# From octet 2 on: every product as two outputs on two 64-row halves of the array

## The chip, the cores and the metric

The kernel runs on one core of one Trainium2 chip. Five engines work side by side and meet through semaphores: TensorE (PE; its weight loads are listed apart as PEld), VectorE (DVE), ScalarE (ACT), GpSimd (POOL) and SyncE (SP), which here only issues transfers. The metric is the device time of one execution in microseconds (us), shown as the median of several runs. The profile is of one execution; its span reaches from the first to the last instruction of the program.

## The reference

A token mixer and an MLP read the same normalised input, and both results are added to the input (S = 2048 tokens, D = 448, 16 heads of 28, F = 1792):

```python
xn = layernorm(x)
# branch A, "hedgehog" linear attention
q, k, v = split(xn @ wqkv)                        # 16 heads of 28
phi_q = concat(softmax(q @ w_phi), softmax(-q @ w_phi))   # per head, 56 wide
phi_k = the same of k
kv  = phi_k^T @ v          # per head, 56 x 28, summed over all tokens
z   = sum over tokens of phi_k
A   = ((phi_q @ kv) / (phi_q . z + 1e-6)) @ wo
# branch B
h   = gelu(layernorm(xn) @ w1)                    # 448 columns in four groups of 112
hs  = (groups of h moved by +1, -1, +2, -2 tokens) @ w2
x1  = xn + hs
B   = x1 + gelu(layernorm(x1) @ w3) @ w4
out = x + A + B
```

## The kernel before

The tokens are 16 tiles of 128. A helper class, `Recorder`, takes down every operation in the order in which the Python code names it, works out which operation must wait for which from the memory that they touch (`solve`), and then hands each engine its own operations in that order. So the order of the calls is the order on every engine, and an engine that waits holds up all that was recorded behind it. All matrix products have the line of the helper `mm` (L188), transposes on TensorE that of `tr` (L192), ScalarE's work that of `act` (L196), VectorE's and GpSimd's that of `ew` (L200).

*Contraction over 448 rows.* Weights and transposed activations lie in four overlapping blocks of 128 rows that begin at rows 0, 128, 192 and 320. The product for an even tile takes blocks 0, 3 and 2 whole (`full`) and the upper 64 rows of block 1 (`tail`), one for an odd tile blocks 0, 3 and 1 and the lower 64 rows of block 2. That is three and a half passes over the array. `batch` puts the tails of several outputs next to each other, so that those of an even and an odd tile use the two halves of the array.

*Accumulators.* There are eight banks, `banks[0]` to `banks[7]`, used in pairs by `two(b)`. Each call names its bank. `nxt` turns three pairs over for k and q, and w2's products of the tiles 4 to 7 have the single banks 6 and 7 in turn.

*The stages.* `octet(g)` handles four tiles g of v and of w1 (`v_pair`, `w_pair`), 0 and 1 first, then 2 and 3 with the folds between. A fold multiplies w_phi into the weights of k or q (`fold`), 112 columns a product. `w2_tile` makes w2's product of four groups of 112 rows, adds it into `xn` on VectorE (`w2_add`) and takes the statistics of the sum there. Then `ks` and `qs` make phi(k) and phi(q): each pair of tiles ends in two exps on ScalarE (scale +1 and -1), and `k_norm` sums and inverts per head on VectorE and multiplies on GpSimd. `kv_tile` accumulates kv over all tokens with 64-column weights, two at once. `chunks` makes two of the 14 columns' blocks of w3 for four tiles, ending in one gelu; `plan` lists nine batches of them with what stands between. `num_tile` is the numerator: eight products of 120 columns per tile, a chain of six operations on VectorE, two on GpSimd; then `o_T` transposes its result by a transfer. `fin_full`, `fin_tail` and `fin_out` are the last product with w4 and wo, and the sum. The exp and the gelu need different tables on ScalarE, loaded by `table`. Transposes by transfer (`xn_Td`, `h_T`, `g_T`, `eq_T`, `o_T`) are all issued by SyncE, one after the other.

Of the kernel before, what the change touches and what calls it, by code (L numbers as in the profile page):

```python
# [6 lines left out]
ALU = mybir.AluOpType  # L7
# [10 lines left out]
class Recorder:  # L18
# [5 lines left out]
    def __init__(self, nc, es):  # L24
        self.nc = nc
        self.es = es
        self.ops = []
        self.rows = {}

# [36 lines left out]
    def op(self, eng, fn, outs, ins, dma=False):  # L66
# [6 lines left out]
        self.ops.append((eng, fn, w, r, dma))  # L73

    def solve(self):
# [8 lines left out]
        for eng, fn, w, r, dma in self.ops:  # L84
# [4 lines left out]
            need = {}  # L89
# [96 lines left out]

    def mm(self, out, lhsT, rhs, start, stop):
        self.op("PE", lambda e: e.matmul(out, lhsT, rhs, start=start, stop=stop, skip_group_check=True),  # L188
                [out], [lhsT, rhs])

    def tr(self, out, in_, ident):
        self.op("PE", lambda e: e.transpose(out, in_, ident), [out], [in_, ident])  # L192
# [16 lines left out]
def bass_parallel_sum__linear_kernel_hedgehog__mixer_s_mlp__prompt_kernel(  # L209
# [9 lines left out]
    QE = DH + 2  # L219
    PAD = 16  # L220
# [4 lines left out]
    with es:  # L225
# [58 lines left out]
        kvq = new("kvq", 8 * 128).rearrange("p (b e) -> p b e", b=8)  # L284
        kvT = view(wpk_r, NC * 224).rearrange("p (c f) -> p c f", c=NC)
# [81 lines left out]
        mb = maskb[0:CR, :].rearrange("p (h e) -> p h e", h=4)  # L367
        vp = vaug.rearrange("p t (h e) -> p (t h) e", e=HP)
        kvq = kvq[:, :, 0:4 * QE]
        kq = kvq[0:CR, :, :].rearrange("p b (h e) -> p b h e", e=QE)  # L370

        def table(name):
# [16 lines left out]
        R.ew(pool, "memset", maskb[0:CR, :], 1.0)  # L389
        R.op(pool, lambda e: e.affine_select(mb, mb, pattern=[[-DH, 4], [0, DH]], compare_op=ALU.is_ge,  # L390
                                             fill=0.0, base=0, channel_multiplier=1), [maskb[0:CR, :]], [maskb[0:CR, :]])
        R.op(pool, lambda e: e.affine_select(mb, mb, pattern=[[DH, 4], [0, DH]], compare_op=ALU.is_ge,
                                             fill=0.0, base=DH - 1, channel_multiplier=-1),
             [maskb[0:CR, :]], [maskb[0:CR, :]])

        def pads(r, n, at):
            t = view(r, n * 128, at=at).rearrange("p (m d) -> p m d", d=128)
            R.ew(pool, "memset", t[:, :, CR:128], 0.0)
# [3 lines left out]
        def late_3():  # L402
            for b in range(8):
                R.ew(pool, "tensor_copy", kq[:, b, :, DH + 1:DH + 2], mb[:, :, 0:1])
# [48 lines left out]

        def spin(n, cols):
            for _ in range(n):
                R.mm(banks[3][:, 0:cols], busy[:, 0:128], busy[:, 0:cols], True, True)

        def fold(t, m, b, eng):
            b = banks[b]
            for c in range(NC):  # L460
                R.mm(b[:, CR * c:CR * c + CR], wT[0:CR, t, c, START[m]:START[m] + 128], bd[0:CR, c, :, 0:DH], True, True)
            dst = wpq if t == 0 else wpk
            if eng == "ACT":
                R.act(dst[:, m, :], b[:, 0:D], ACT.Copy)
            else:
                R.ew(eng, "tensor_copy", dst[:, m, :], b[:, 0:D])

        def xn_T(i, b):
            b = banks[b]
            for kc in range(KC):  # L470
                R.tr(tview(b)[:, 128 * kc:128 * kc + 128], xn[:, i, 128 * kc:128 * kc + 128], ident[:, :])
            R.act(xnT[:, :, 128 * i:128 * i + 128], tview(b).rearrange("p (c d) -> p c d", c=KC), ACT.Copy)

# [45 lines left out]
        def q_pair(i, b):  # L519
            def out():  # L520
                r, at = (eq_r, i % 12) if i % 12 < 8 else (hi_r, 4 + i % 12 - 8)
                e = view(r, 2048, at=2048 * at).rearrange("p (t s c d) -> p t s c d", t=2, s=2, c=NC)
                for s in range(2):
                    R.act(e[:, :, s, :, 0:CR],
                          two(b)[:, :, 0:D].rearrange("p t (c d) -> p t c d", c=NC), ACT.Exp, scale=1.0 - 2.0 * s)
# [5 lines left out]

        def batch(last, first=(), between=(), led=()):
            for p, _ in last:
                for o in p:
                    full(o, True)
            for f in between:
                f()
            for i in led:
                fin_tail(i)
            for p, _ in last:  # L540
                for o in p:
                    tail(o, False)
            for p, _ in first:
                for o in p:
                    tail(o, True)
            for i in led:
                fin_out(i)
            for _, out in last:
                out()
            for p, out in first:  # L550
                for o in p:
                    full(o, False)
                out()
# [13 lines left out]
        def kv_tile(i):  # L567
            for c in range(NC):
                b = banks[4 + c // 2][:, 224 * (c % 2):224 * (c % 2) + 224].rearrange("p (s f) -> p s f", s=2)
                for j in range(2):  # L570
                    R.mm(b[64 * j:64 * j + 64, :, 56 * j:56 * j + 56],
                         vaug[:, i, 128 * c + 64 * j:128 * c + 64 * j + 64],
                         phik[:, i, :, CR * c + 56 * j:CR * c + 56 * j + 56],
                         i == 0 and c % 2 == 0, i == NT - 1)

        def kv_copy():
            src = two(4)[:, :, 0:448].rearrange("p h (k f) -> p h k f", f=CR)
            dst = kvT[:, :, :].rearrange("p (h c) (s f) -> p h (c s) f", h=2, s=2)
            for j in range(2):
                r, f = slice(64 * j, 64 * j + 64), slice(56 * j, 56 * j + 56)  # L580
                R.ew(dve, "tensor_copy", dst[r, :, :, f], src[r, :, :, f])

        def kv_blocks(b):
            b = banks[b]
            tv = tview(b, 1024).rearrange("p (b e) -> p b e", b=8)
            for c in range(NC):
                for s in range(2):
                    R.tr(tv[0:CR, 2 * c + s, :], kvT[:, c, CR * s:CR * s + CR], ident[:, :])
            t4 = tv[0:CR, :, :].rearrange("p (c s) (h e) -> p c s h e", s=2, e=HP)
            k4 = kq.rearrange("p (c s) h e -> p c s h e", s=2)  # L590
            for s in range(2):
                R.ew(dve, "tensor_tensor", k4[:, :, s, :, 0:DH + 1], t4[:, :, s, :, 0:DH + 1],
                     mb[:, :, 0:1].unsqueeze(1).to_broadcast([CR, NC, 4, DH + 1]), op=ALU.mult)

        def w2_tile(i, b):
            w2_mul(i, b)
            w2_add(i, b)

        def w2_mul(i, b):
            b = banks[b]  # L600
            for m in range(NM):
                c0 = PAD + 128 * i - SHIFTS[m]
                R.mm(b[:, 0:D], hT[0:CR, m, c0:c0 + 128], w2[0:CR, m, :], m == 0, m == NM - 1)

        def w2_add(i, b, stats=True):
            b = banks[b]
            x1, x = xn[:, i, 0:D], xn[:, i, :]
            x = bass.AP(x.tensor, x.offset, [list(x.ap[0]), [288, 2], [1, 224]])
            R.ew(dve, "tensor_tensor", x1.rearrange("p (h d) -> p h d", h=2),
                 b[:, 0:D].rearrange("p (h d) -> p h d", h=2), x, op=ALU.add)  # L610
# [10 lines left out]
        def num_tile(i, b0):  # L621
            g, j = divmod(i, 4)
            r = i % 2
            bs = [banks[b0], banks[b0 + 1]]
            for s in range(2):
                for c in range(NC):
                    R.mm(bs[s][:, 4 * QE * c:4 * QE * c + 4 * QE], eqT[0:CR, i % 4, s, c, :],
                         kvq[0:CR, 2 * c + s, :], True, True)
            pp, pm = (b[:, 0:H * QE].rearrange("p (h e) -> p h e", e=QE) for b in bs)
            rcpm, rho, dsum, rden = (q_s[:, r, 16 * k:16 * k + 16] for k in range(4))  # L630
            R.ew(dve, "reciprocal", rcpm, pm[:, :, DH + 1])
            R.ew(dve, "tensor_tensor", rho, pp[:, :, DH + 1], rcpm, op=ALU.mult)
            R.ew(dve, "tensor_tensor", q_t[:, r, :, :], pm[:, :, 0:DH + 1],
                 rho.unsqueeze(2).to_broadcast([128, H, DH + 1]), op=ALU.mult)
            R.ew(dve, "tensor_tensor", q_n[:, r, :, :], pp[:, :, 0:DH + 1], q_t[:, r, :, :], op=ALU.add)
            R.ew(dve, "scalar_tensor_tensor", dsum, pp[:, :, DH + 1], DEN_EPS, q_n[:, r, :, DH],
                 op0=ALU.mult, op1=ALU.add)
            R.ew(dve, "reciprocal", rden, dsum)

# [5 lines left out]
            if i >= NT - 2:  # L645
                c0 = 192 + 64 * (i % 2)
                R.ew(pool, "memset", o_tok[:, i % 4, c0:c0 + 64], 0.0)
# [19 lines left out]
        def fin_bank(i):  # L667
            return (0 if i > 13 else 4) + i % 2

        def product(i, b, c):  # L670
            g, j = divmod(i, 4)
            s = slice(128 * j, 128 * j + 128)
            o = b[:, 0:c.stop - c.start]
            for fc in range(FC):
                R.mm(o, h3T[:, g % 2, fc, s], w4[:, fc, c], fc == 0, False)
# [279 lines left out]
```

## Time and profile before

| what | value |
|---|---|
| runs | 180.98 us median of 3 (180.67 to 181.21) |
| the profiled execution | 180.65 us, span 178.9 us |
| TensorE products | 173.8 us busy, 1198 recorded |
| weight loads | 89.3 us busy, 1206 recorded |
| VectorE | 117.2 us busy |
| GpSimd | 94.4 us busy |
| ScalarE | 79.5 us busy |

Products are pipelined: a row's busy time runs over the start of the next, so the distance of two starts is the pace and not the busy time. A few records are missing (1198 products stand against 1206 weight loads); where a first product is missing, the row starts one product late. In a shape such as `64*128 64x448`, the first numbers are the rows and columns of the array that are used, the last is the number of columns streamed. A row that says `<-PE bank` waited for TensorE to finish a bank. The buffers' names are those of the memory they lie in: `phik` also holds the MLP's hidden activations, `vaug` the numerators and the output, `hi` and `eq` the exps of q, and `w` is any of w1 to w4.

### The profile page before, as it was taken

Reading aid. Unit: us, or ns where it says so; the run is one execution under the profiler, and the core shown is the slowest. Engines: PE = TensorE matmul, PEld = TensorE weight load, DVE = VectorE, ACT = ScalarE, POOL = GpSimd, SP = SyncE. Lnnn points to the kernel's source line nnn. Section 1 sums busy time; section 2 is a strip of 40 time slices with the busy share of each in tenths; the row PEclk is TensorE's granted clock in tenths of the full one; section 3 lists DMA queues with packets and bytes.
Section 4 is the critical chain, followed back from the end, with each engine's and each line's share of the span. In section 5 each row is a group of like instructions: output and inputs, shape, how many; then the busy total and the mean of one; then the engine's idle time right before and its main releaser. Section 6 shows DMA issues by size and latency. Waiting matters only on the chain.

```text
span 178.9 us, 3153 instructions
## 1 busy us (share of the span) xinstructions
PE 173.8 (97%) x1198; PEld 89.3 (50%) x1206; DVE 117.2 (65%) x270; ACT 79.5 (44%) x97; POOL 94.4 (53%) x146
## 2 busy tenths in 40 slices
PE   7899999999999999999999999999999999999994
PEld 4454555444446344644644654553644644645564
DVE  4899979459999999584594295195272352655531
ACT  2378881889999459768005004103206006014000
POOL 6885680077999797002458527037835063151660
PEclk9999999999999999999999999999999999999999
DMA  5999554469795479583247444552554755030231
GB/s 161 339 222 176 80 106 88 81 122 285 206 199 86 101 196 280 100 157 60 59 88 92 86 90 91 134 64 59 114 114 99 106 114 115 24 60 28 55 106 51
DMA packets 60774, 21.44 MB, mean 120 GB/s; under 512 B 52376, under 2 KB 60248, under 8 KB 60760
## 3 DMA queue, kind: packets, MB, share of 16 engines
q1 hardware_dynamic: 56910, 16.94, 49.5%
q10 hardware_dynamic: 3850, 4.31, 8.1%
q8 instruction: 9, 0.15, 0.4%
q14 instruction: 5, 0.04, 0.1%
HBM read 7.08 MB, written 1.84 MB: 50 GB/s over the span
## 4 chain that ended last, share of the span: by engine, by line
PE 89%; DVE 7%; issue 2%; POOL 1%; ACT 0%
PE bank L188 88%; DVE vaug L200 3%; DVE st L200 2%; PE bank L192 1%; DVE xn L200 1%; DVE mv L200 1%; POOL rs L200 0%; ACT xnT L196 0%; DVE gT L200 0%; POOL mv L200 0%
## 5 line engine op out<-in xcount | busy, mean ns | idle before, releaser
L196 ACT ACTIVATE phik<-bank 128x1024 bf16<-128x1024 f32 (+1 forms) x44 | 40.2, 991 | 68.0 <-PE bank L188 67.9
L188 PE MATMUL bank<-w,phik 128*128 128x448 bf16 (+2 forms) x238 | 45.2, 342 | 0.0
L188 PE MATMUL bank<-gT,w 128*128 128x512 bf16 (+1 forms) x216 | 44.1, 379 | 0.8 <-DVE vaug L200 0.3
L200 DVE TENSOR_TENSOR vaug<-bank,vaug 128x464 f32<-128x464 f32 (+3 forms) x65 | 33.1, 514 | 17.4 <-PE bank L188 13.5
L200 POOL TENSOR_TENSOR xnT<-vaug 128x196 bf16<-128x196 f32 (+1 forms) x32 | 18.1, 585 | 48.9 <-DVE vaug L200 48.9
L188 PEld LDWEIGHTS bank<-w,phik 128*128 128x128 bf16 x238 | 22.6, 98 | 18.4 <-issue 0.2
L188 PEld LDWEIGHTS bank<-gT,w 128*128 128x128 bf16 (+1 forms) x224 | 18.0, 97 | 24.2 <-issue 5.1
L200 POOL TENSOR_TENSOR phik<-phik,rks 128x896 bf16<-128x896 bf16 x15 | 25.8, 1754 | 1.0 <-DVE rks L200 0.9
L200 DVE TENSOR_TENSOR xn<-bank,xn 128x448 bf16<-128x448 f32 x16 | 9.6, 599 | 11.6 <-PE bank L188 11.5
L200 POOL TENSOR_TENSOR vaug<-xn,xtok 128x448 f32<-128x448 bf16 x16 | 16.4, 1030 | 1.4 <-DVE vaug L200 1.4
L200 DVE TENSOR_REDUCE ksum<-phik 128x32 f32<-128x896 bf16 x16 | 16.6, 1036 | 0.0
L200 POOL TENSOR_TENSOR rs<-mv,mhalf 128x2 f32<-128x2 f32 (+1 forms) x19 | 15.0, 788 | 1.5
L200 DVE RECIPROCAL vaug<-bank 128x16 f32<-128x16 f32 x16 | 3.7, 228 | 17.8 <-PE bank L188 17.8
L188 PE MATMUL bank<-wo,xnT 128*128 128x448 bf16 (+3 forms) x68 | 14.7, 343 | 0.0
L188 PE MATMUL bank<-w,hT 112*128 112x448 bf16 x64 | 14.2, 352 | 0.0
L188 PE MATMUL bank<-wv,xnT 128*128 128x448 bf16 (+1 forms) x64 | 14.0, 354 | 0.1
L188 PE MATMUL bank<-w,xnT 128*128 128x448 bf16 (+1 forms) x64 | 13.9, 352 | 0.0
L188 PE MATMUL bank<-wpk,xnT 128*128 128x448 bf16 (+1 forms) x64 | 12.2, 353 | 0.0
L188 PE MATMUL bank<-wpq,xnT 128*128 128x448 bf16 (+1 forms) x64 | 12.1, 354 | 0.0
L200 POOL TENSOR_SCALAR mv<-mv 128x4 f32<-128x4 f32 x4 | 0.8, 202 | 19.4 <-DVE mv L200 19.4
L196 ACT ACTIVATE eq<-bank 128x896 bf16<-128x896 f32 x12 | 10.0, 923 | 1.4 <-PE bank L188 1.4
L200 DVE BATCH_NORM_STATS2 st<-xn 128x6 f32<-128x448 bf16 x16 | 9.9, 620 | 0.4
(65 smaller groups left out, 173.9 us busy)
## 6 DMA issues: line engine op xcount, KB each, us to landing
w<-in_B_w_dram ACTq DMA_DIRECT2D x2, 896.0 KB, 5.3
out_dram<-vaug SPq DMA_DIRECT2D x15, 112.0 KB, 1.9
w<-in_B_w_dram ACTq DMA_DIRECT2D x1, 1568.0 KB, 9.7
xtok<-in_A_x_dram SPq DMA_DIRECT2D x2, 448.0 KB, 7.1
wo<-in_A_wo_dram SPq DMA_DIRECT2D x2, 224.0 KB, 3.6
w<-in_B_w_dram SPq DMA_DIRECT2D x1, 392.0 KB, 4.2
hi<-eq SPq DMA_TRANSPOSE x24, 2.5
xtok<-in_A_x_dram SPq DMA_DIRECT2D x3, 112.0 KB, 2.6
```

What stands on the lines that cost most here:

```text
L188: self.op("PE", lambda e: e.matmul(out, lhsT, rhs, start=start, stop=stop, skip_group_check=True), [out], [lhsT, rhs])
L192: self.op("PE", lambda e: e.transpose(out, in_, ident), [out], [in_, ident])
L196: self.op("ACT", lambda e: e.activation(out, in_, func, **kw), [out], [in_] + aps)
L200: self.op(eng, lambda e: getattr(e, name)(out, *args, **kw), [out], aps)
```

## The change

From octet 2 on, every product with 128 weight columns is made by one half of the array, 64 rows, while the other half makes another output.

- `duo` gives the two outputs of a pair seven steps. In each step one output is on one half and the other on the other half; after four steps (three for the second part) they change halves. `w2_tile` splits its 448 columns into two outputs of 224, `fold` does two blocks, `product` does two token tiles in 35 steps.
- A bank that has been written by one half is written by the other only after the first one's last product is done. `_pe` finds these places and adds a wait of TensorE on itself. To fill them, `task` records the first part of a task, then the second part of the task before it, and then the evacuation of that one. `flush` records a second part at once.
- The accumulators are now four pairs in a list, `free`. `take` gives out the one that has been free longest, and it comes back when its evacuation is recorded. kv holds one pair from `kv_tile(0)` to `kv_copy`.
- phi(q) is laid out as eight blocks of two heads (56 of 64 columns), so that `num_tile` makes 16 products of 60 columns on two halves in place of 8 of 120. kv is made by single heads: 16 products of 56 columns with 32-column weights per tile, four at once, in place of 8 of 112.
- The order around these is new: in the k/q stage w2's tiles and `k_norm` stand elsewhere, two output tiles are finished at a time, and the last two tiles in two column parts (0 to 352, 352 to 448).

```diff
+    def _pe(self, fn, out, lhsT, rhs):
...
+        if mode == (True, False):
+            row = lhsT.offset * DTB[lhsT.dtype] // self.rows[lhsT.tensor.name][0]
+            for k in self._keys(out):
+                last = self.group.get(k)
+                if last and last[0] != row:
+                    after = max(after or 0, last[1])
+                self.group[k] = (row, self.npe)
+        self.npe += 1
+        self.op("PE", fn, [out], [lhsT, rhs], after=after)
...
+        free = [0, 2, 4, 6]
+        def take():
+            return free.pop(0)
+        def task(b, steps, cut, out):
+            def phase(some):
+                for both in some:
+                    for a in both:
+                        R.mm(*a)
+            phase(steps[:cut])
+            flush()
+            wait.append((lambda: phase(steps[cut:]), out, lambda: free.append(b)))
+        def flush():
+            while wait:
+                for f in wait.pop():
+                    f()
+        def whole(pair, i, *a):
+            b = take()
+            p = pair(i, b)
+            task(b, duo(p[0]), DUO, lambda: p[1](*a))
...
+        def duo(p):
+            one = [[(kc, 0) for kc in (0, 3, 2, 1)] + [(kc, 64) for kc in (0, 3, 2)],
+                   [(kc, 64) for kc in (0, 3, 1, 2)] + [(kc, 0) for kc in (0, 3, 1)]]
+            return [[(out, lhs(o[n][0], o[n][1], o[n][1] + 64), rhs(o[n][0], o[n][1], o[n][1] + 64), n == 0, n == 6)
+                     for (out, lhs, rhs, _), o in zip(p, one)] for n in range(7)]
...
         def kv_tile(i):
...
+                for k in range(4):
+                    h = 8 * (k // 2) + 2 * c + k % 2
+                    R.mm(b[HP * k:HP * k + HP, :, :], vaug[:, i, HP * h:HP * h + HP], phik[:, i, :, DH * h:DH * h + DH],
+                         i == 0 and c == 0, i == NT - 1)
...
+        def w2_tile(i, stats=True):
+            b = take()
+            steps = []
+            for n in range(2 * NM):
+                m = n % NM
                 c0 = PAD + 128 * i - SHIFTS[m]
+                both = []
+                for h in range(2):
+                    lo, hi = ((0, 64), (64, CR))[(h + n // NM) % 2]
+                    both.append((banks[b + h][:, 0:DS], hT[lo:hi, m, c0:c0 + 128], w2[lo:hi, m, DS * h:DS * h + DS], n == 0,
+                                 n == 2 * NM - 1))
+                steps.append(both)
+            task(b, steps, NM, lambda: w2_add(i, b, stats))
...
-        def num_tile(i, b0):
+        def num_tile(i):
+            b0 = take()
...
+                    for k in range(2):
+                        p, at = slice(64 * k, 64 * k + 2 * DH), QE * (8 * s + 2 * c)
+                        R.mm(banks[b0 + k][:, at:at + 2 * QE], eqT[p, i % 4, s, c, :], kvq[p, 2 * c + s, :, :], True, True)
...
+            free.append(b0)
...
+        whole(v_pair, 8, "ACT")
+        xn_Th(11)
+        whole(w_pair, 8)
+        whole(v_pair, 10, "ACT")
+        fold(1, 0, "DVE")
+        whole(w_pair, 10)
+        fold(1, 2, "ACT")
...
+        ks(0, 2)
         load_w3(0)
+        fold(0, 0, "DVE")
+        fold(0, 2, "DVE")
+        ks(4, 6)
         for i in range(4):
             g_apply(i)
             g_T(i)
         k_norm(0)
         k_norm(2)
+        W(4)
+        qs(0, 2)
+        k_norm(4)
+        k_norm(6)
         load_w3(1)
+        ks(8, 10)
         for i in range(4):
             eq_T(i)
+        W(5)
+        k_norm(8)
+        qs(4, 6)
+        k_norm(10)
         h_T(11)
+        W(6)
+        ks(12, 14)
+        W(7)
+        flush()
         ln_scale(mv2, rs2, 4, 4, 4)
...
         k_norm(12)
         k_norm(14, dve)
...
+        def late_w2():
+            w2_tile(9, False)
+            w2_tile(10, False)
+            N(0)
+            E(4)
+            O(0)
+            flush()
...
+            (w3s, 3), (load_w4,),
+            (w3s, 3), (flush,), (table, "exp_and_others"), (ga, 1, dve), (load_wo,), (qs, 8, 10), (W, 8), (kv, 8, 16), (kv_copy,),
+            (qs, 12, 14), (flush,), (table, "gelu_apprx_tanh_and_others"), (kv_blocks,), (late_w2,),
+            (w3s, 4), (N, 1), (E, 5), (O, 1), (W, 11), (N, 2), (E, 6), (O, 2), (flush,), (sc, 2), (N, 3), (E, 7), (O, 3), (F2, 0),
...
+            (w3s, 3), (N, 15), (O, 15), (flush,), (F2, 12)]
...
+        last(0, 352)
         x_sum(15)
+        last(352, D)
+        flush()
```

In the list, `w3s` n is n pairs of w3 blocks, N a numerator, E and O the transposes of phi(q) and of the numerator's result, W a w2 tile, `F2` i the last product of the tiles i and i + 1, `ga` and `sc` the second layernorm of four tiles.

More of the change, by code (lines that the diff above doesn't have):

```diff
@@ L472, in xn_T, with xn_Th @@
             R.act(xnT[:, :, 128 * i:128 * i + 128], tview(b).rearrange("p (c d) -> p c d", c=KC), ACT.Copy)
+        def xn_Th(i):
+            b = take()
+            for kc in range(KC):
+                for h in range(2):
+                    p = slice(64 * h, 64 * h + 64)
+                    R.tr(tview(banks[b + h])[:, 64 * kc:64 * kc + 64], xn[p, i, 128 * kc:128 * kc + 128], ident[p, p])
+            src = pairs[b // 2][:, :].bitcast(BF16).rearrange("p (h e) -> p h e", h=2)[:, :, 0:64 * KC]
+            dst = xnT[:, :, 128 * i:128 * i + 128].rearrange("p c (h s) -> p h c s", h=2)
+            R.act(dst, src.rearrange("p h (c s) -> p h c s", c=KC), ACT.Copy)
+            free.append(b)
         def xn_Td(i):
@@ L855, in bass_parallel_sum__linear_kernel_hedgehog__mixer_s_mlp__prompt_kernel, with w3s @@
         table("gelu_apprx_tanh_and_others")
+        kvb.append(take())
         for i in range(8):
             kv_tile(i)
[L859 to L863 removed]
+        E, O, F2, N = eq_T, o_T, fin, num_tile
+        def w3s(n):
+            for _ in range(n):
+                whole(chunks, done[0])
+                done[0] += 2
         def ga(g, eng=pool):
@@ L920, in bass_parallel_sum__linear_kernel_hedgehog__mixer_s_mlp__prompt_kernel, with last, out @@
+        for step in plan:
+            step[0](*step[1:])
+        assert done[0] == 4 * FC
+        def last(c0, c1):
+            def out(i, b):
+                R.ew(dve, "tensor_tensor", outb[:, 2:4, c0:c1], two(b)[:, :, 0:c1 - c0], xs[:, :, c0:c1], op=ALU.add)
+                for k in range(2):
+                    R.dma(out2d[128 * (14 + k):128 * (15 + k), c0:c1], outb[:, 2 + k, c0:c1], ("SP", "ACT")[k])
+            product(14, c0, c1, out)
+        last(0, 352)
+        x_sum(14)
         x_sum(15)
-        for c, b, e in ((slice(0, 256), 1, "SP"), (slice(256, D), 2, "ACT")):
-            product(15, banks[b], c)
-            R.ew(dve, "tensor_tensor", outb[:, 3, c], banks[b][:, 0:c.stop - c.start], xs[:, 1, c], op=ALU.add)
-            R.dma(out2d[128 * 15:, c], outb[:, 3, c], e)
+        last(352, D)
```

329 lines of the change are left out of this document (133 added, 196 removed).

## The prediction

> **What bounds the kernel now.** I read the page first (shares, slices, chain), then TensorE's timeline, then VectorE, ScalarE and SyncE where TensorE would run into them.
>
> ```profile
> span 178.9 us, 3153 instructions
> ...
> PE 173.8 (97%) x1198; PEld 89.3 (50%) x1206; DVE 117.2 (65%) x270; ACT 79.5 (44%) x97; POOL 94.4 (53%) x146
> ...
> PEclk9999999999999999999999999999999999999999
> ...
> PE 89%; DVE 7%; issue 2%; POOL 1%; ACT 0%
> ```
>
> TensorE (PE) is busy 97% of the span, at full granted clock, and 89% of the chain is its own. So a first sum counts TensorE's time alone, and a second asks what it will then wait for. This profiled execution took 180.65 us, 1.75 outside its span and 0.33 under the median of 180.98.
>
> Timeline rows (start, busy, tile, shape, count; neighbours merged), the stage of k and q first:
>
> ```profile
> 31.00 0.36 PE L188 MATMUL bank<-wv,xnT 64*128 64x448 bf16 x2
> 31.20 0.35 PE L188 MATMUL bank<-w,xnT 64*128 64x448 bf16 x2
> ...
> 34.90 3.03 PE L188 MATMUL bank<-wpk,xnT 128*128 128x448 bf16 x16
> ...
> 41.42 0.92 PE L188 MATMUL bank<-w,hT 112*128 112x448 bf16 x4
> 42.17 3.02 PE L188 MATMUL bank<-wpq,xnT 128*128 128x448 bf16 x16
> 45.04 3.02 PE L188 MATMUL bank<-wpk,xnT 128*128 128x448 bf16 x16
> ...
> 55.99 1.76 PE L188 MATMUL bank<-phik,vaug 128*64 128x112 bf16 x64
> ```
>
> ```profile
> 65.88 1.47 PE L188 MATMUL bank<-gT,w 128*128 128x512 bf16 x6
> 67.19 3.02 PE L188 MATMUL bank<-wpq,xnT 128*128 128x448 bf16 x16
> 70.05 0.92 PE L188 MATMUL bank<-w,hT 112*128 112x448 bf16 x4
> 70.90 1.76 PE L188 MATMUL bank<-phik,vaug 128*64 128x112 bf16 x64
> 72.59 3.03 PE L188 MATMUL bank<-wpq,xnT 128*128 128x448 bf16 x16
> ...
> 77.43 0.58 PE L188 MATMUL bank<-kvq,hi 112*128 112x120 bf16 x8
> ...
> 88.50 1.00 PE L188 MATMUL bank<-kvq,hi 112*128 112x120 bf16 x16
> 89.34 2.81 PE L188 MATMUL bank<-w,phik 128*128 128x448 bf16 x14
> ```
>
> Differences of starts give the pace. Four hT products: 0.75, so 0.189 for 448 columns; 512 columns: 1.31 / 6 = 0.218, less a last shape change 0.216. Two half-row products run at once: pairs start 0.20 apart. A q batch (42.17 to 45.04) is 12 full products and 2 pairs, 14 x 0.189 = 2.65, and takes 2.87: going to half rows and back costs 0.2.
>
> **The change, on TensorE alone.** *Shape changes:* 20 round trips vanish (octets 2 and 3, six in the k/q stage, two q batches, nine chunk batches, the last tails); kv's two stay, half a trip is added at octet 2. 19.5 x 0.2 = 3.9 saved. *Two outputs on two halves:* 7 pair steps replace 7 full equivalents, at the same 0.189; weight loads double, but the pairs above load two per step at that pace, so 0. w2 (8 steps of 224 columns for 4 of 448) and folds: 0. *phi(q) numerators:* 16 products took 0.84 (88.50 to 89.34), 0.42 per token tile; now 8 steps of 60 columns, half the time by columns, 0.22. If issuing sets the pace, the nearest row is kv's, 64 products in 70.90 to 72.59 less 0.1, 0.025 each: 16 x 0.025 = 0.40. Between 0.3 and 3.2 saved over 16 tiles; I take 3.2, because kv's own pace equals its columns (112 in 0.049 per pair). *kv:* 128 products of 56 columns, four at once, replace 64 of 112: 0.8 by columns, 3.2 by 0.025 per product, where 1.6 was. I take 0.9 per eight tiles, near the column end for the same reason: 1.4 saved in both. *A wait of TensorE on itself* between a task's two halves: the record puts another task's half between (0.38 or more), and a reader starts 0.21 after a stream's end, so 0; if it were exposed it would be 0.2 at some 80 tasks. Sum: 180.65 - 8.5 = 172.2.
>
> **What is late next: the banks.** Every task now takes one of four pairs in the order freed, so it reuses the pair of the fourth task before, and its first product waits until that one's evacuation has read it. Before, w2 tiles 4 to 7 had banks 6 and 7 to themselves. Rows of VectorE and ScalarE in the k/q stage:
>
> ```profile
> 39.69 1.16 DVE L200 CAST wpq<-bank 128x448 bf16<-128x448 f32 x2 [0.37 <-PE bank L188]
> 40.77 1.07 DVE L200 TENSOR_REDUCE ksum<-phik 128x32 f32<-128x896 bf16 x1
> ...
> 46.14 0.56 DVE L200 TENSOR_TENSOR xn<-bank,xn 128x448 bf16<-128x448 f32 x1
> ...
> 47.50 1.05 DVE L200 TENSOR_REDUCE ksum<-phik 128x32 f32<-128x896 bf16 x1
> ...
> 52.86 0.56 DVE L200 TENSOR_TENSOR xn<-bank,xn 128x448 bf16<-128x448 f32 x1
> ```
>
> ```profile
> 35.00 1.28 ACT L373 ACT_TABLE_LOAD   x1
> 36.54 1.73 ACT L196 ACTIVATE phik<-bank 128x896 bf16<-128x896 f32 x2 [0.26 <-PE bank L188]
> ...
> 40.19 3.35 ACT L196 ACTIVATE phik<-bank 128x896 bf16<-128x896 f32 x4 [0.31 <-PE bank L188]
> ```
>
> Four tiles of k_norm cost VectorE 5.37 (40.77 to 46.14), 1.34 each; a w2 sum with its statistics 1.36. Two exps of a pair cost ScalarE 1.73, 1.6 in a row.
>
> *k/q stage,* 0 at the first k product. k0 ends after 11 steps, 2.08; its exps run 2.3 to 4.0. k4 takes k0's pair and starts at 4.07; fold 2's second half follows at 5.03, its casts end at 6.3. Then VectorE's order is four tiles (to 11.7), W4's sum and statistics (13.05), and, because k_norm(8) is now recorded before the step that finishes W5, six tiles instead of four: 13.05 + 8.05 = 21.1, and W5's sum ends at 21.65. TensorE (1.32 per k or q pair, 0.77 per W, 0.4 for two folds, waits of 0.85, 0.65, 0.4 and 0.1 for the pairs of k4, k6, k10, W6) is at k12 at 18.2. k12 takes W5's pair, so it waits 3.5, with all of TensorE's queue behind it. k12, W6, k14, W7 then end at 25.5. Before: 55.99 - 34.90 = 21.1. So +4.4; 0.9 if VectorE were in time.
>
> *Octets 2 and 3.*
>
> ```profile
> 19.84 0.73 PE L188 MATMUL bank<-wv,xnT 128*128 128x448 bf16 x3
> ```
>
> ```profile
> 18.15 2.58 SPq L203 DMA_TRANSPOSE xnT<-xn  x2
> ```
>
> ```profile
> xnT<-xn SPq DMA_TRANSPOSE x7, 2.5
> ...
> xnT<-xnT SPq DMA_TRANSPOSE x16, 2.4
> ```
>
> Token tile 9's transpose is issued at 18.15 and lands 2.5 later, at 20.65. v8's first step now needs tiles 8 and 9 at once and TensorE comes at 19.94: 0.7 of wait. Less the two round trips (0.4), and 0.1 for the shape change at the start: +0.4.
>
> *kv and six chunk pairs.* 0.9 for 1.6, two round trips less (0.4), 0.2 of wait for W6's sum, 0.1 of other waits: before 67.19 - 55.99 = 11.2, now 10.45, -0.75.
>
> *q8 to chunk pair 6.*
>
> ```profile
> 65.56 2.85 ACT L196 ACTIVATE phik<-bank 128x1024 bf16<-128x1024 f32 x3 [1.89 <-PE bank L188]
> 68.43 1.28 ACT L373 ACT_TABLE_LOAD   x1
> ```
>
> ScalarE sets this one. Counted from the last chunk half, its gelu ends at 1.5 (0.92 apart), the table at 2.8, q8's exps at 4.5, q10's at 6.1. TensorE, done with q8, q10, W8 and kv at 4.05, waits for q8's pair (q12), then for q10's (q14, 6.16); q12's exps end at 9.4, q14's at 11.0. W10 takes q12's pair, numerator 0 takes q14's (11.1). Chunk pair 6 starts at 11.7; before, 77.43 + 0.42 - 67.19 = 10.65. +1.0, whatever the kv term within 1 us.
>
> *The rest.*
>
> ```profile
> 84.73 0.26 DVE L200 RECIPROCAL vaug<-bank 128x16 f32<-128x16 f32 x1 [2.41 <-PE bank L188]
> ```
>
> ```profile
> 87.13 1.13 POOL L200 TENSOR_TENSOR xnT<-vaug 128x280 bf16<-128x280 f32 x2 [5.55 <-DVE vaug L200]
> ```
>
> ```profile
> 1.26 4.23 PE L188 MATMUL bank<-gT 128*128 128x256 bf16 x19 [1.26 <-DVE gT L200]
> ```
>
> ```profile
> 172.91 1.69 PE L188 MATMUL bank<-w,phik 128*128 128x256 bf16 x14
> ...
> 174.88 1.32 PE L188 MATMUL bank<-w,phik 128*128 128x192 bf16 x14
> 176.03 0.49 PE L188 MATMUL bank<-wo,xnT 128*128 128x192 bf16 x4
> ```
>
> Before: 77.85 to 176.36, 98.5. Now 22 chunk pairs x 1.512 + 7 products of two tiles x 35 x 0.189 + the last 6.7 + five w2 x 0.77 + 15 numerators x 0.22 = 93.4. New waits: numerator 3 takes numerator 1's pair (0.55), and the first product needs oT of tile 1 as well as 0: VectorE 2.4, POOL 1.15, transpose 2.4 behind numerator 1, some 6.4, where TensorE comes after 5.3 (1.1). 95.1: -3.4. The end: two adds and stores of two column parts, +0.2.
>
> Sum: 180.65 + 0.4 + 4.4 - 0.75 + 1.0 - 3.4 + 0.2 = 182.5.
>
> The Trainium skill, TensorEngine Tiling (Array Packing), section PSUM Bottleneck, speaks against the change in general: tiling speeds up TensorE but not PSUM evacuation, which may become the bottleneck. By TensorE's rows alone the sum is 172.2, with the evacuations as that section would have it, 182.5; the rows of VectorE above say where.
>
> **Rivals.** *VectorE is in time (other side).* If W5's sum has been made before TensorE asks for its pair, the k/q stage costs 22.0 and the whole 179.0. It decides at a wait of 1.65 in place of 3.5, that is the sum by 19.8. For it: before, the sum ended 18.5 after the first k product (34.90 to 53.42). Against: VectorE works in recorded order. 0.2. *TensorE stays the bound,* 172.2 to 176: needs ScalarE's table and exps between chunk pairs 5 and 6 out of the way as well. 0.06. *kv goes by issue,* 3.2 per eight tiles: +2.3 in each of the two stages less 0.9 of waits it covers: 186.2. Against it: the column pace. 0.1. *The clock drops in the 3.5 us stop.* At the start 19 products of 256 columns took 4.05, 0.213 each; at the end 18 took 1.97, 0.109. Four us at the slow pace lose 2: 184.5. Against it: every slice shows the full granted clock, though no stop here is as long. 0.08. The Trainium skill, TensorE: Matmul & The Clock Gate, Part 1, has the clock halved after an idle window of about 3.4 us; by that rule this rival is the case, and no row here can show it.
>
> **How the numbers follow.** The forecast, slower by 181.3 to 184, has 0.5; 0.06 falls between it and the faster cases. A measurement tells about 0.3% (0.5 us) from no change. Faster: 0.2 + 0.06 = 0.26; same 0.06; slower 0.5 + 0.1 + 0.08 = 0.68. The range leaves out the full gain and part of the kv case: 178 to 186.2; the forecast's own is 181.3 to 184.
>
> **What would show it.** Right: TensorE idle about 3.5 us before a wpk pair some 18 us after the first, released by VectorE's xn sum; a short stop before numerator 0 released by ScalarE; half-row pairs at 0.189; numerators at 0.22; no change of shape outside kv. Wrong: that idle time under 1.6, kv's eight tiles far from 0.9, steps slower than 0.189, or waits of TensorE for itself.

## The result, and the profile after

The changed kernel took 187.31 us (median of four executions), the kernel before 180.85 beside it: a ratio of 1.0346, with a 95% interval of 1.0323 to 1.0369. The direction was forecast, the size was not: 182.5 was predicted, with 178.0 to 186.2 as the range. One execution at 194.02, with a granted clock of 0.973 over its span, is left out of the ratio; where a kernel below scatters in the same way, its range is given. The profiled one took 186.98, 185.3 of it span.

Five parts of its page (span, busy shares, granted clock, the queue that brings the engines' code, the chain):

```profile
span 185.3 us, 5420 instructions
...
PE 168.3 (91%) x2334; PEld 105.1 (57%) x2334; DVE 117.7 (64%) x271; ACT 81.4 (44%) x97; POOL 92.3 (50%) x137
...
PEclk9999999999999999999999999999999999999999
...
q8 instruction: 18, 0.29, 0.8%
...
PE 61%; DVE 16%; ACT 5%; DMA 5%; issue 4%; POOL 3%; SPq 3%; DVEq 0%; ACTq 0%
```

TensorE is busy 5.5 us less than before (173.8), and its share of the chain has gone from 89% to 61%. It now has 2,334 products, each with a weight load, where it had 1,198. What it waits for (us in total, times, the longest):

```profile
PE bank L207 <- DVE xn L218: 4.4, 3, 3.3
PE bank L207 <- issue: 1.8, 1, 1.8
PE bank L210 <- DVE xn L218: 1.2, 2, 0.9
...
PE bank L207 <- ACT phik L214: 1.2, 2, 0.7
PE bank L207 <- PE bank L207: 1.0, 1, 1.0
PE bank L207 <- DMA hi<-in_A_wqkv_dram: 1.0, 1, 1.0
PE bank L207 <- DMA xnT<-xnT: 0.7, 1, 0.7
```

"Issue", a stop for which no semaphore is late, was in no term of the sum, and TensorE waiting for itself was a term put at 0. In what follows k12 and q12 are the k and q products of the tiles 12 and 13, W5 is the w2 product of tile 5, c0 or chunk pair 0 the first pair of w3 blocks. Rows of TensorE's timeline (start, busy, tile, shape, count, and the idle time before with its releaser):

```profile
34.98 0.35 PE L207 MATMUL bank<-wpk,xnT 64*128 64x448 bf16 x1
...
53.13 0.73 PE L207 MATMUL bank<-wpq,xnT 64*128 64x448 bf16 x6
57.17 0.93 PE L207 MATMUL bank<-wpk,xnT 64*128 64x448 bf16 x8 [3.30 <-DVE xn L218]
...
61.21 1.21 PE L207 MATMUL bank<-phik,vaug 128*32 128x56 bf16 x128
64.22 2.12 PE L207 MATMUL bank<-gT,w 64*128 64x512 bf16 x18 [1.79 <-issue]
...
73.29 2.24 PE L207 MATMUL bank<-wpq,xnT 64*128 64x448 bf16 x22
...
77.88 0.93 PE L207 MATMUL bank<-wpq,xnT 64*128 64x448 bf16 x8
79.77 0.56 PE L207 MATMUL bank<-w,hT 48*128 48x224 bf16 x8 [0.96 <-PE bank L207]
...
85.79 5.58 PE L207 MATMUL bank<-gT,w 64*128 64x512 bf16 x50
...
91.19 0.40 PE L207 MATMUL bank<-kvq,hi 56*128 56x60 bf16 x16
91.41 0.56 PE L207 MATMUL bank<-w,hT 64*128 64x224 bf16 x8
...
93.94 2.81 PE L207 MATMUL bank<-w,phik 64*128 64x448 bf16 x28
96.59 0.35 PE L207 MATMUL bank<-wo,xnT 64*128 64x448 bf16 x1
...
156.42 1.88 PE L207 MATMUL bank<-w,phik 64*128 64x448 bf16 x18 [0.68 <-ACT phik L214]
```

The stages, by the starts of their first products ("the rest" ends with the last product's stream), with the prediction's figure between:

| stage | before | predicted | after |
|---|---|---|---|
| start to first k product | 34.90 | 35.3 | 34.98 |
| k and q stage (to kv's first burst) | 21.09 | 25.5 | 26.23 |
| kv and six chunk pairs (to q8) | 11.2 | 10.45 | 12.08 |
| q8 to chunk pair 6 | 10.65 | 11.7 | 12.50 |
| the rest, to the last product | 98.5 | 95.1 | 96.3 |
| the end | 2.5 | 2.7 | 3.2 |

The profiled execution is 4.5 above the forecast: 0.7 in the k and q stage, 1.6 behind kv, 0.8 in the q8 stage, 1.2 in the rest, 0.5 at the end, less 0.3 at the start.

### The profile page after: what moved, and what is told of

Its sections match the earlier page's. It is cut to its first block, busy times and chain, and to the rows that moved or that the text cites. A ratio compares the mean times of both kernels' runs of the same rounds, so it can differ in the third digit from the quotient of the medians.

```text
span 185.3 us, 5420 instructions
## 1 busy us (share of the span) xinstructions
PE 168.3 (91%) x2334; PEld 105.1 (57%) x2334; DVE 117.7 (64%) x271; ACT 81.4 (44%) x97; POOL 92.3 (50%) x137
## 4 chain that ended last, share of the span: by engine, by line
PE 61%; DVE 16%; ACT 5%; DMA 5%; issue 4%; POOL 3%; SPq 3%; DVEq 0%; ACTq 0%
PE bank L207 61%; DVE ksum L218 5%; ACT phik L214 3%; SPq L221 3%; DVE vaug L218 3%; DVE xn L218 2%; DVE st L218 2%; DMA hi<-in_A_wqkv_dram 2%; POOL rs L218 2%; DMA xnT<-xn 1%; DMA xnT<-xnT 1%; DVE wpq L218 1%; DVE rks L218 1%; ACT hi L214 1%; DVE mv L218 1%
## 5 line engine op out<-in xcount | busy, mean ns | idle before, releaser
L207 PE MATMUL bank<-gT,w 64*128 64x512 bf16 x392 | 46.7, 376 | 1.8 <-issue 1.8
L207 PE MATMUL bank<-w,phik 64*128 64x448 bf16 (+2 forms) x504 | 46.0, 329 | 0.7 <-ACT phik L214 0.7
L207 PEld LDWEIGHTS bank<-w,phik 64*128 64x128 bf16 x504 | 26.2, 94 | 16.2 <-ACT phik L214 0.8
L207 PEld LDWEIGHTS bank<-gT,w 64*128 64x128 bf16 x392 | 20.7, 94 | 20.1 <-issue 1.9
L207 PE MATMUL bank<-w,hT 64*128 64x224 bf16 (+1 forms) x256 | 17.5, 256 | 1.6 <-PE bank L207 1.0
L207 PE MATMUL bank<-wpk,xnT 64*128 64x448 bf16 x112 | 12.6, 350 | 4.1 <-DVE xn L218 3.6
L207 PEld LDWEIGHTS bank<-w,hT 64*128 64x128 bf16 (+1 forms) x256 | 12.8, 94 | 5.5 <-PE bank L207 1.4
L207 PE MATMUL bank<-wo,xnT 64*128 64x448 bf16 (+2 forms) x126 | 14.6, 329 | 0.7 <-DMA xnT<-xnT 0.7
L207 PE MATMUL bank<-wv,xnT 64*128 64x448 bf16 (+1 forms) x88 | 14.1, 351 | 0.3 <-DMA xnT<-xn 0.2
L207 PE MATMUL bank<-w,xnT 64*128 64x448 bf16 (+1 forms) x88 | 14.1, 350 | 0.0
```

The lines of the kernel that those rows point to most:

```text
L207: self._pe(lambda e: e.matmul(out, lhsT, rhs, start=start, stop=stop, skip_group_check=True), out, lhsT, rhs)
```

## The experiments

**Which stop is code?** Behind kv's first burst nothing that the first chunk needs was late: the exps of its bank pair had ended at 61.6, its transposes landed by 53.8. But one packet of 16 KB of instructions was fetched from 61.31 to 62.83 (below, the instruction queue from 61.3 to 62.9), and the stop ended 1.38 later; in q tiles 12 and 13 the same from 77.32 to 78.42 and 1.35.

```profile
q8 instruction: 1, 0.02, 6.0%
```

Theory A says that kv's 256 instructions (128 products and their loads) run in about 1 us while a fetch needs nearly 3 from its first packet to its use (61.31 to 64.21); theory B looks for late data or a bank. Two runs tell them apart, one moving only where the fetches fall, one making the burst half as many instructions.

```diff
-            spin(19, 256)
+            spin(76, 64)
```

> The changed kernel with the 19 opening products of 256 columns written as 76 of 64 columns: the same columns at the start, 114 more TensorE instructions (57 products, each with its weight load) ahead of everything else, and nothing else moved. Theory A (code): in the changed kernel TensorE stands still for 1.8 us between kv's first burst and the first chunk, and for 1.3 us in the middle of q tiles 12 and 13, with no semaphore late; in both places 16 KB of instructions were fetched just before (61.31 to 62.83, stop ends 64.21; 77.32 to 78.42, stop ends 79.77: 1.38 and 1.35 us after the fetch), and 256 kv instructions run in about 1 us where a fetch needs nearly 3. A fetch follows each 256 instructions or so, so 114 more ahead put the fetches elsewhere against the bursts: the first stop falls from 1.8 to under 0.5, the second from 1.3 to under 0.5, and the time from 187.0 to between 183 and 185. Theory B (data or banks: the first chunk waits for the gT transposes, w3 or the exps of k12 to k14, and q12's second half for its pair): nothing here changes those, both stops stay, time within 0.5 of 187.0.

```diff
...
-                for k in range(4):
-                    h = 8 * (k // 2) + 2 * c + k % 2
-                    R.mm(b[HP * k:HP * k + HP, :, :], vaug[:, i, HP * h:HP * h + HP], phik[:, i, :, DH * h:DH * h + DH],
+                for k in range(2):
+                    h = 8 * k + 2 * c
+                    R.mm(b[64 * k:64 * k + 64, :, :], vaug[:, i, HP * h:HP * h + 64], phik[:, i, :, DH * h:DH * h + 2 * DH],
...
```

> The changed kernel with kv in 64 products of 64 weight columns by 112 columns per eight tiles, as before the change, instead of 128 of 32 by 56, in the same bank layout but for the columns between. Theory A (code): the burst is 128 TensorE instructions in 1.7 us (kv's row of before: 64 products in 1.6 to 1.7) instead of 256 in 1.0, so a fetch of 256 instructions has time: the stop behind the first burst (1.8) and the one in q tiles 12 and 13 (1.3) go, kv itself costs 0.65 more each time. In the first place -1.15; in the second TensorE is then held by ScalarE's exps of q8 to q14 (79.45 instead of 81.70 for the start of q12's), so up to -2. Time 184 to 185.5. Theory B (data or banks): stops stay as long as their data are late; kv 0.65 longer is hidden in the first stop: 187.0 to 187.7.

TensorE's timeline of the first, where only the code was shifted:

```profile
57.25 1.67 PE L207 MATMUL bank<-wpk,xnT 64*128 64x448 bf16 x8 [3.26 <-DVE xn L218]
...
63.76 1.36 PE L207 MATMUL bank<-phik,vaug 128*32 128x56 bf16 x128
65.28 1.04 PE L207 MATMUL bank<-gT,w 64*128 64x512 bf16 x8 [0.16 <-issue]
...
78.95 0.93 PE L207 MATMUL bank<-wpq,xnT 64*128 64x448 bf16 x8
79.72 0.55 PE L207 MATMUL bank<-w,hT 64*128 64x224 bf16 x8
```

And of the second, with kv's wider products:

```profile
63.01 1.76 PE L207 MATMUL bank<-phik,vaug 128*64 128x112 bf16 x64
64.71 1.47 PE L207 MATMUL bank<-gT,w 64*128 64x512 bf16 x12
```

Both stops are gone in both runs, with the order of all data and banks as it was: from kv's start to the first chunk 1.52 and 1.70 us instead of 3.01, from q8 to chunk pair 6 11.86 and 11.85 instead of 12.50. The fetches bear it out: with the code shifted they fell at 54.27 to 55.20 and 65.53 to 66.46, on either side of the burst; with the wider products one still fell into it (63.38 to 64.54), but TensorE had work until the block was there. Theory B falls. Code thus cost 1.5 in the first place and 0.65 in the second, where a wait for ScalarE took part of the gain (0.30 in the first run): 2.1 us by the stages.

Yet the times were 187.18 (ratio 1.0329, 1.0282 to 1.0377) and 187.50 (1.0356, 1.0316 to 1.0396), not 183 to 185.5. In the profiled executions the 2.1 us were given back elsewhere, most of it ahead of kv. Busy time per stretch of the changed kernel (PE, PEld, DVE, ACT, POOL, then the granted clock of TensorE):

```profile
57.00:60.00 3.00, 2.83 (x38) 1.86 (x40) 2.90 (x6) 0.14 (x1) 3.00 (x3) 1.00 0.44 89
```

and of the run with shifted code:

```profile
53.00:57.00 4.00, 1.00 (x14) 0.46 (x10) 3.90 (x7) 3.19 (x4) 4.00 (x4) 0.84 0.40 72
57.00:60.00 3.00, 2.75 (x20) 1.48 (x22) 2.90 (x6) 0.00 (x0) 3.00 (x2) 0.50 0.56 115
60.00:64.00 4.00, 4.00 (x70) 2.12 (x64) 2.14 (x6) 1.67 (x3) 3.42 (x3) 0.68 0.49 102
```

In the stop for VectorE, of the same length in both, the clock fell to half in one and stayed full in the other. k12's first half then took 1.67 instead of 0.93, and from k12 to kv it was 6.51 us instead of 4.04: 2.5 lost (1.55 in the second run, where the clock fell at 57.63, just behind the stop). The second run lost another 0.9 in the rest, with a second wait for an oT transpose (0.6). The clock is not all, though: one of its executions took 187.30 at full clock, and there is no trace of that one. So these two runs show what the stops cost by stage, and not what they are worth in time. The changed kernel's two other executions near the median have a mean clock of 0.991 where its profiled one has 0.999; the kernel before was at 1.000 in these comparisons.

**Is it W5's sum?** The prediction put the loss on one recorded line. The next run moves that line alone, the one after moves the next normalisation too (both edits are against the changed kernel).

```diff
-        k_norm(8)
         qs(4, 6)
+        k_norm(8)
         k_norm(10)
```

> The changed kernel with the normalisation of k tiles 8 and 9 recorded behind q tiles 4 to 7 instead of ahead of them, so that VectorE makes W5's sum after four tiles of k_norm and not six. The prediction's price: the 3.5 us stop before k tiles 12 and 13 is the loss, and goes; its rival with VectorE in time put the kernel 3.5 us lower: 183.5. The other theory: VectorE has no idle time from 39.7 to 71 us, and kv's bank pair waits for W6's sum, which stands behind the same sums and normalisations as now in either order (61.16 us): the stop before k12 shrinks to under 1 us and a stop of about 2.7 us appears ahead of kv, with the time within 0.5 of 187.0.

```diff
-        k_norm(8)
         qs(4, 6)
+        k_norm(8)
-        k_norm(10)
         h_T(11)
         W(6)
         ks(12, 14)
+        k_norm(10)
         W(7)
```

> As the run before (k_norm of tiles 8 and 9 behind q tiles 4 to 7), and the normalisation of k tiles 10 and 11 behind k tiles 12 to 15 as well, so that W6's sum too comes two tiles (2.67 us) earlier on VectorE. If VectorE's order is what holds kv back, kv starts 2.6 us earlier, at 58.6 instead of 61.2, and the time is 184.4; the stop behind kv's first burst stays (code is not touched) unless ScalarE's exps of k12 to k14 hold the first chunk. If the whole amount of VectorE's work, and not its order, holds the stage (rival: kv then waits for a normalised tile of POOL or DVE), 186 to 187.

The first, TensorE's timeline:

```profile
54.98 0.93 PE L207 MATMUL bank<-wpk,xnT 64*128 64x448 bf16 x8 [0.64 <-DVE xn L218]
...
61.68 1.45 PE L207 MATMUL bank<-phik,vaug 128*32 128x56 bf16 x128 [2.73 <-DVE xn L218]
63.26 2.98 PE L207 MATMUL bank<-gT,w 64*128 64x512 bf16 x26
...
79.33 0.56 PE L207 MATMUL bank<-w,hT 48*128 48x224 bf16 x8 [1.47 <-issue]
```

The stop of 3.3 shrank to 0.64, and one of 2.73 appeared ahead of kv: 186.57 (1.0332, 1.0294 to 1.0370), no gain that these intervals show. kv's bank pair is W6's, and W6's sum stands behind the same four tiles as before. (The stop for code behind kv's first burst is gone here too: the fetch was done, 59.52 to 60.70, while TensorE stood ahead of kv. The one behind the second burst stays: 1.47.) In the second run W6's sum came earlier as well:

```profile
59.42 1.35 PE L207 MATMUL bank<-phik,vaug 128*32 128x56 bf16 x128
62.53 3.84 PE L207 MATMUL bank<-gT,w 64*128 64x512 bf16 x34 [1.75 <-issue]
```

Counted from the first k product, kv starts after 23.45 instead of 26.23: 2.8 us, as expected of VectorE's order. The time fell only to 186.12 (1.0303, 1.0258 to 1.0348), not to 184.4. The first k product came 1.0 later (35.97; octet 2 waits for its xnT transposes, whose landing differs between executions), and the rest took 97.5 instead of 96.3, with a second wait for an oT transpose that the changed kernel does not have.

**Do the two causes add?** The same order with the wider kv products:

> Two edits of before together: VectorE's sums first (k_norm of tiles 8 to 11 behind, as e4) and kv in 64 products of 112 columns per eight tiles (as e2). In e4 kv started 2.8 us earlier counted from the first k product, but the stop of 1.75 us for code stayed behind the first burst; in e2 that stop was gone and kv with its stop took 1.70 instead of 3.00. If the two are separate costs, they add: e4's 186.1 less 1.3 is 184.8. With no stop of TensorE above 1 us left, the granted clock should be full in all runs and these lie within 0.5 us of each other (in e1 and e2, whose stop of 3.3 us stayed, the profiled clock fell to 0.5 in it and k tiles 12 to 15 ran at half pace, which cost 2.6 and 1.7 us). If something else takes the place (ScalarE's exps of k12 to k14 hold the first chunk), 185.5 to 186.2.

TensorE's timeline of kv and the first chunk:

```profile
58.35 1.76 PE L207 MATMUL bank<-phik,vaug 128*64 128x112 bf16 x64
60.05 1.25 PE L207 MATMUL bank<-gT,w 64*128 64x512 bf16 x10
```

183.04 (1.0109, 1.0070 to 1.0148), better than expected, in part since the first k product came at 35.07 in this one. The k and q stage took 23.28, kv to the first chunk 1.70, q8 to chunk pair 6 11.85, and after the opening no stop above 0.9 is left. All four executions were at full clock. So the two causes together explain about 4 of the 6.3 us by which the change was slower by its ratio: 4.3 by the ratios, 4.0 between the two profiled executions, with a clock of 0.999 and 1.000.

**Is the rest order, or half rows?** The remaining runs keep the work of the change and write a new order from the k and q stage on. The first has the wider kv, the second the change's own. Both put fold 2 behind the first k pair, spread kv's tiles among the chunks, and put w2 tiles 9 and 10 between the last q pairs.

> The changed kernel with its work as it is, but a new order of recording from the k and q stage to the end (W sums ahead of normalisations on VectorE, first fold between k tiles, kv's tiles spread among chunks and q tiles, w2 tiles 9 and 10 between the last q pairs, F2 and numerators further apart), and kv in 112-column products. If it was the order, and neither half rows nor the pair ring as such, that cost the time, every stage comes near its TensorE time: k and q stage 21.5 (26.2 in the changed kernel), q8 to chunk pair 6 about 10.3 (12.5), the rest 95.3 (96.3), kv 0.5 dearer than in narrow products: about 180.0. If half-row products or the four-pair ring cost time of their own that only moves about, 183 or more.

> As the run before, with kv in 32-column weights by 56 columns as in the change, in pieces of at most five tiles (160 instructions) with other work between. If a stop for code needs a burst that uses up 256 instructions in less than a fetch of some 3 us, pieces of 160 leave at most a stop below 1 us in one place, and kv's 1.1 us are saved again: 179.0 to 180.0. If any burst of small products stops TensorE, it has two or more stops of 1 to 2 us marked as issue: 181 to 183.

Neither came near: 185.85 (1.0246, 1.0185 to 1.0308), and 184.47 to 188.80 for the second, whose executions scatter too much for a ratio. By the limit set for the first, 183 or more, half rows or the ring of four pairs would cost time of their own; but the traces name waits that these orders brought in, so the two runs settle nothing of the kind. TensorE's timeline of the second says why, followed by the granted clock of one stretch:

```profile
38.02 0.22 PE L207 MATMUL bank<-bd,hi 64*128 64x112 bf16 x2 [1.85 <-DMA hi<-in_A_wqkv_dram]
38.52 0.28 PE L207 MATMUL bank<-bd,hi 64*128 64x112 bf16 x2 [0.28 <-DMA hi<-in_A_wqkv_dram]
38.59 2.82 PE L207 MATMUL bank<-wpk,xnT 64*128 64x448 bf16 x14
...
43.48 1.49 PE L207 MATMUL bank<-wpk,xnT 64*128 64x448 bf16 x14
...
62.84 0.24 PE L207 MATMUL bank<-phik,vaug 128*32 128x56 bf16 x8 [0.49 <-issue]
```

```profile
39.00:40.00 1.00, 1.00 (x8) 0.41 (x6) 0.00 (x0) 0.04 (x1) 1.00 (x2) 0.50 0.33 66
```

A fold was asked for before its wT transposes had landed, and behind it 14 half products took 2.82, where the same count takes 1.49 at full clock, at 43.48. Later, group 3's gT transposes stood on SyncE behind others that waited (2.5 us of TensorE in the first run, 1.4 in the second). The 128 kv products, cut into pieces of at most 80, still stopped once for code, 0.49. The next two orders, with the wider kv, avoid that. The plain fence has the first of them, without loads, copies, scalings and transposes: k and q for the first tile of a pair, g for g_apply, norm for k_norm, c for a chunk pair, N for a numerator tile, P for a product of two tiles.

```
k2 k4 g0-3 fold2 k10 fold0 norm2 k0 norm4 k14 W4 q0 q2 norm0 k6 W6 k8 q6 norm6 W7 k12 norm10 q4 W5 (gelu)
kv0 kv1 norm8 kv2-5 c0 c1 kv6 kv7 c2-4 norm12 kv8 c5 kv9 norm14 (exp) kv10 kv11 q8 W8 kv12 g4-7 kv13-15
q10 W9 q12 W10 q14 c6 N0 (gelu) W11 c7 c8 N1 c9 N2 c10 N3 P0 N4 N5 W14 c11 W13 g8-11 c12 N6 P2 W15 c13 W12 ...
```

> A second new order from the k and q stage on, with kv in 112-column products and the last two tiles in columns 0 to 255 and 256 to 447. What the first new order (e6, e7) got wrong is taken out: its first fold is not asked for before the wT transposes have landed (it stood 2.1 us there), group 3's gT transposes are no longer queued on SyncE behind transposes that wait (TensorE stood 2.7 us), and no stop is planned that is long enough for the clock to fall (it fell behind both of these stops). If the change's loss is order alone, the k and q stage takes 21.5 to 22, q8 to the first chunk pair after numerator 0 no wait above 0.5, the rest 93.5 to 95, the time is 177 to 179 and the clock is full in all runs. If half-row products cost what no order can hide, it stays above 180.85, the kernel before the change.

> Another order of the same kind, which keeps the first k and q steps nearer to the changed kernel's (folds behind k tiles 0 to 3) and has short waits left (0.3 to 0.7 at six places by the rows of the changed kernel): 177.5 to 179.5 if the loss is order alone, above 180.85 if it is not.

The first took 179.89 (median of ten), the kernel before 180.74: 0.9940 (0.9910 to 0.9970), 0.6% faster than the kernel before, though not the 177 to 179 expected. The second, with 177.5 to 179.5 expected, lay between 180.13 and 186.66; in its profiled execution a fold waited 3.4 us for a wT transpose, the clock fell to half in that wait and stayed there for 6.8 us, and no ratio is given. The last run takes the first of these orders with the change's own kv.

> The order of the run that beat the kernel before (e8), with one edit: kv in 32-column weights by 56 columns, as the change has it, in pieces of one to four tiles (at most 128 instructions) with chunks and q tiles between. By columns it saves 2 x 0.5 us of TensorE. If bursts so short never use up 256 instructions within a fetch, there is no stop for code, and the time falls from 179.9 by up to 1.0 (less where ScalarE's exps and gelus hold TensorE in those stretches anyway: 179.4 then). If the pieces still stop for code, they stop behind two or three of them, and the time stays at 179.9 or rises.

```profile
span 177.4 us, 5422 instructions
...
PE 168.8 (95%) x2334; PEld 103.8 (59%) x2334; DVE 117.7 (66%) x271; ACT 81.5 (46%) x97; POOL 93.4 (53%) x137
...
PE 56%; DVE 18%; POOL 10%; DMA 9%; SPq 3%; issue 2%; ACTq 0%; DVEq 0%
```

```profile
58.40 0.68 PE L207 MATMUL bank<-phik,vaug 128*32 128x56 bf16 x64
59.19 2.65 PE L207 MATMUL bank<-gT,w 64*128 64x512 bf16 x22
...
71.51 0.39 PE L207 MATMUL bank<-phik,vaug 128*32 128x56 bf16 x32
73.14 0.39 PE L207 MATMUL bank<-phik,vaug 128*32 128x56 bf16 x32 [1.24 <-POOL phik L218]
```

179.01 us against 181.30 for the kernel before beside it: 0.9890 (0.9856 to 0.9924), the best of all. Every product of the change is in it (only the last pair of tiles is cut at column 256 instead of 352, as in the kernel before), no piece of kv stops for code for more than 0.3, and it has the changed kernel's TensorE time, 168.8 to 168.3. The chain is TensorE's to 56% all the same: kv's tile 14 now waits for POOL's normalisation, the saved half microsecond of kv became a wait there, and 172.2, the sum by TensorE alone, is far. The narrow kv against the wide one (0.9890 to 0.9940, intervals that overlap) is not settled as a gain. What is shown is that half rows as such did not make the change slower: the same products in another order are 1.1% faster than the kernel before. Whether a new order alone would have done as much for that kernel, whose TensorE stood idle for 5.1 us of its span, was not tried.

## Why the prediction was right and wrong

**TensorE's own terms held where they can be read.** Numerators: 16 products in 0.22 (91.19 to 91.41). Half-row steps: 14 in 2.65 (93.94 to 96.59), 0.189 each. kv: 1.02 for the first eight tiles and 1.18 for the second, where 0.9 was taken. The rival "kv goes by issue" ended nearest to the time, 186.2, by another road: the bursts were near their columns (0.8) and far from its 3.2. The 8.5 saved in all is not shown: TensorE's busy time fell by 5.5.

**The k and q stage: right on the stop, incomplete on its cause.** The stop stood where it was said to be (ahead of k12, 18.9 us after the first k product, 3.30 idle, ended by VectorE's xn sum), and the stage came out at 26.23 for 25.5; part of the difference is fold 0's wait for wT (0.96 idle), which is no term of the sum: k4 came 4.48 after the first k product, not 4.07. But the step "VectorE's six tiles instead of four" and the rival "VectorE in time: 179.0" took W5's sum for the whole price. Taking it away gained nothing clear; the next sum in the same queue, W6's, held kv to the same end. Both had to move, for 2.8 us.

**kv and six chunk pairs: the step that failed.** "Now 10.45" counted columns and waits; for the doubled loads the sum asked only for their pace ("so 0"), and the arrival of the code was in no term. The weight and product count per eight tiles had doubled, to 256 instructions, in 0.6 of the time. Measured: 12.08, of which 1.5 is the stop for code; without it 10.6, close to the forecast. With the 0.65 of the next stage, code is 2.1 of the 4.5 us of the miss, its largest part.

**q8 to chunk pair 6.** 11.7 forecast, 12.50 measured, 11.85 without the stop for code. ScalarE was a bound of this stage as said (0.64 idle for q's exps, at 83.48), but the short stop right before numerator 0 (0.77) ended with VectorE's xn sum, where the prediction named ScalarE.

**The rest.** Of the two waits named, numerator 3's cost 0.6 (0.55 said) and the first product's oT 0.85 (1.1 said). Not seen was a third: two numerators taken in a row between chunk pair 24 and product 10 use up two bank pairs in 0.45 us, so that the product asks for a pair whose gelu is not done (0.85 between starts, 0.68 of it idle, at 156.42). By difference, TensorE's sum there was some 0.6 short as well. The end cost 0.7 instead of 0.2: the last add waits for the add of 352 columns, and the last store is issued behind the store of that part.

**The clock rival** ("four us at the slow pace lose 2", 0.08) did not happen in the profiled execution of the change and did in those of two other runs: 2.5 and 1.55 us. The clock records of the traces say when it can happen: the clock changes only at multiples of 3.41 us after its first rise (4.56, then 55.76 and 62.59 with the code shifted; 4.41, then 38.55 and 41.96 in the seventh run), so that half clock lasted 3.41 or 6.83 us in all five profiled executions in which it fell among the products. The Trainium skill, TensorE: Matmul & The Clock Gate, Part 1, has the clock halve after an idle window of about 3.4 us that runs freely, not from the kernel's start. That a stop of one length halves it in one execution and not in another agrees with a free window. That the window must be idle throughout does not agree: a mean of 0.84 over 53 to 57 is half clock from about 55.7, 1.7 us into the stop that began at 53.99, and in the seventh run it was at half after 1.85 and 0.28 us of idle time, with TensorE busy earlier in the same 3.41 us. What lowers it in one case and not in another stays open.

## What to carry to other kernels

Small products on parts of the array save columns but multiply instructions per microsecond: count these per burst, and set longer products between pieces of a burst of some hundreds. When a wait in a shared, in-order queue is removed, look which item of that queue is waited for next before booking the gain: here two sums had to move for one of them to count. And a stop of TensorE of two or three microseconds can cost more than its length: the clock can halve in it or behind it. Kernels with such stops scattered by one to four per cent here, more than the clock alone takes: the ninth run's executions at 0.991 and at full clock lie 3.4 us and more apart, where 3.41 us at half clock lose 1.7 at most.

## What the hardware showed that was not expected

TensorE can stand still with every semaphore in place. Its code arrives in blocks of 16 KB (18 of them in the changed kernel, 9 before), one for about each 256 of TensorE's instructions; kv's 256 ran in 1.0 us, and TensorE then stood 1.79 us, until 1.38 us after the block's last packet. The Trainium skill, Runtime: NRT & Kernel Launch, Instruction fetch mechanics, states blocks of 256 instructions, which the trace bears out, and that their fetch is hidden because instructions are issued more slowly than blocks arrive; in this burst (some 4 ns per instruction) it is not. Whether it shows depends on where in the program a block's edge falls: 114 more instructions at the very start took away a stop of 1.5 us in the middle.
